# V of the second attention laid out one head over 128 partitions, PV on 128x32 tiles, shared buffer pools, and loads that read 8192 B at once

## The chip, the cores and the metric

The kernel runs on one core of a Trainium2 chip. Its time is the device time of one execution in microseconds (us). A difference is judged on the median of several runs. The profile that is shown is of one execution of the program.

## The reference, cut to what matters

Two attention blocks with cached keys and values are computed on inputs of their own, and their outputs are joined along the last axis. They differ in the number of key heads: the first has 4, each shared by 8 query heads, the second has 32, one for each query head. All inputs are bfloat16.

```python
# first (A): B, Sq, D = 16, 32, 1024; Hq, Hkv, Sk, Dh = 32, 4, 1024, 128
# second (B): the same with H = 32 heads in k_cache and v_cache
q = (x @ wq).reshape(B, Sq, Hq, Dh).transpose(0, 2, 1, 3)
k, v = repeat(k_cache, Hq // Hkv, axis=1), repeat(v_cache, Hq // Hkv, axis=1)
p = softmax(einsum("bhqd,bhkd->bhqk", q, k) * Dh ** -0.5)
o = einsum("bhqk,bhkd->bhqd", p, v)
out = o.transpose(0, 2, 1, 3).reshape(B, Sq, Hq * Dh) @ wo
# result: concatenate([out_A, out_B], axis=-1)
```

K and V of the second attention are 134.2 MB each, those of the first 16.8 MB each. The four weights are 8.4 MB each, x and the result are small. Everything is read once: some 338 MB.

## The kernel before, in words

**Quads.** The work on each attention is cut into 128 quads of 128 score rows: 4 heads or batch entries of 32 queries each, against 1024 keys. A quad of the first attention is 4 query heads that share a key head. A quad of the second takes 2 batch entries and 2 of 4 neighbouring heads (heads e and e + 2 for e = 0, 1), so each of its four groups of 32 rows has keys and values of its own. Two quads of the second attention (e = 0 and 1) make a pair, and `pairB(n)` (line 1209) writes its steps out; `quadA_all` (line 1239) does so for a quad of the first. The main loop (line 1331) goes over 128 steps and puts a quad of each, and parts of the projections, into each step.

**Steps of a quad.** Scores by TensorE into two banks of PSUM (`st_scoresA` line 995, `st_scoresB` line 1027 on 32x32 tiles); row maximum by VectorE (line 1038); exponential with row sum by ScalarE into a buffer P (line 1051); transposes of P by TensorE, two bfloat16 values as one float32 (`st_ptr` line 1063, `st_ptB` line 1097); copy from PSUM into a buffer PT (line 651, on ScalarE or VectorE); PV, the product with the values (`st_pvA` line 1083, `st_pvB` line 1116); scaling by the reciprocal of the row sum into a buffer O (lines 1174 and 1175); a transpose of O (line 1182, line 1190 for the second attention) and a copy into OTA_sb or OTB_sb (line 651); and, once a group of heads is complete, the output projection (line 823) with addition to an accumulator (lines 835 and 844). K of the first attention is transposed by TensorE (line 969), that of the second in place by VectorE (line 976).

**V of the second attention before.** A load (`st_dmaVB`, line 955) brings 512 KB: two neighbouring heads of one batch entry, each over 64 partitions, 16 keys or 4096 B in each partition. Six such tiles lie in VB_sb. PV is done for the pair at once, on four tiles of 64x64: 64 rows of keys, 64 columns of queries (two heads at a time), against 256 columns, the values of both heads. Half of that product belongs to the other head. The unwanted half is left out when O is transposed, by two products with a matrix `rowsel` that holds the identity's rows of one head each:

```python
# line 1116, for c in 16 chunks, t_ in 2 batch entries, q in the pair (e0 = 64 * q.e, n0 = 64 * t_)
last = e.matmul(bank(q.vbo)[n0:n0 + 64, 0:2 * Dh]..., pt2_chunk(vPT, c, e0, n0),
                v2[e0:e0 + 64, :, c, :], start=(c == 0), stop=(c == 15), tile_position=(e0, n0))
# line 1190
for i in range(2):
    last = e.matmul(bank(vb)[:, 256:384], O2_sb[:, vO.idx, i, :], rowsel[:, i, :], start=(i == 0), stop=(i == 1))
```

The last pair has a step of its own (`st_last`, line 1123), which goes over the values in two halves (line 1135); its values lie in tiles of K that are free by then. In the last part of the run V and K also use space of xT_sb, QT_sb and wq_sb that is free by then.

**Buffers.** The quads of the first attention have two P, two PT and two O of their own; a pair of the second has one double P (`P2`), two PT of half the keys for both quads (`PT2`) and three double O (`O2`). PSUM has eight banks that all steps share.

**Loads.** All come from the queue of SP, in order: a load waits at the head of the queue until the last reader of its buffer is done, and what stands behind it waits too. K of the second attention comes in 512 KB tiles of 4096 B rows (line 910, eight tiles in KB_sb), K and V of the first in 256 KB with 2048 B rows (lines 891 and 898, two buffers each), output weights in 256 KB with 2048 B rows (lines 795 and 805), x likewise (line 659), query weights in 512 KB with 2048 B rows (line 714). The outputs go out from GpSimd's queue (line 847) and, the last ones, from SP's (line 841).

**Order.** A planner in the kernel (`list_schedule`, line 249) sets the order of the instructions on each engine when the program is built. It simulates the engines with durations from a table (`DUR`), charges TensorE for going into and out of tiled matmuls (`PE_MODE`, `MODE_IN`, `MODE_OUT`), the loads by their row length (`PACKET`) and their issue (`DMA_ISSUE`), lets SP run at most 5 us ahead of the loads (`SP_AHEAD`), and gives out the buffers of each pool (`SLOTS`) as they come free. Its priorities come from a list of variants (`RANKS`), of which `TUNE` picks one for every 77 operations.

Of the kernel before, what the change touches and what calls it, by code (L numbers as in the profile page):

```python
# [7 lines left out]
ALU = alu_op_type.AluOpType  # L8
# [8 lines left out]
NVB_SLOTS = 6  # L17
XT_FREE = 54
LATE = 51
# [11 lines left out]
PE_MODE = {"scoresB": 2, "Qshuf": 2, "Qshuf2": 2, "PVB": 3, "PVBh": 3}  # L31
MODE_IN = 0.094
MODE_OUT = {0: 0.0, 2: 0.18, 3: 0.1}
PE_INSTR = {"scoresB": 32, "scoresA": 2, "PT_trA": 8, "PT_trB": 8, "PVA": 16, "PVB": 32, "PVBh": 32, "OT_tr": 2, "OT_trB": 4, "KTA_tr": 16, "Qshuf": 16, "Qshuf2": 16,
# [12 lines left out]
TUNE = (6, 7, 1, 5, 6, 8, 8, 8, 8, 8, 8, 11, 5, 15, 1, 9, 0, 1, 5, 1, 7, 14,  # L47
        15, 12, 12, 10, 12, 12, 15, 3, 12, 14, 7, 13, 13, 13, 13, 13, 7, 6, 10, 1, 12, 10,
        3, 12, 0, 11, 9, 12, 7, 13, 12, 11, 12, 3, 4, 10, 14, 9, 9, 10, 4, 0, 0)
# [11 lines left out]
    "scoresB": (0.232, 0.20), "scoresA": (0.216, 0.20), "PT_trA": (0.48, 0.22), "PT_trB": (0.48, 0.22), "PVA": (0.45, 0.22), "PVB": (0.437, 0.22), "PVBh": (0.22, 0.22),  # L61
    "OT_tr": (0.056, 0.22), "OT_trB": (0.112, 0.22), "KTA_tr": (0.45, 0.22), "Qshuf": (0.39, 0.20), "Qshuf2": (0.235, 0.20), "qprojA": (0.432, 0.20), "qprojB": (0.432, 0.20),
    "oprojA": (0.432, 0.20), "oprojB": (0.432, 0.20), "xT_tr": (0.45, 0.22),
    "exp": (1.10, 0.12), "PT_ev@act": (0.466, 0.13), "norm@act": (0.25, 0.13), "normB@act": (0.36, 0.13), "OT_ev@act": (0.11, 0.13), "OTB_ev@act": (0.17, 0.13), "KTA_ev@act": (0.466, 0.13),
    "qA_ev@act": (0.47, 0.13), "qB_ev@act": (0.478, 0.13), "QR_ev@act": (0.478, 0.13), "acc0@act": (0.47, 0.13), "acc0@dve": (0.58, 0.12), "xT_ev@act": (0.90, 0.13),
    "o_fin@act": (0.47, 0.13),
    "KBt_tr": (1.15, 0.11), "max": (1.12, 0.11), "recip": (0.06, 0.11), "norm@dve": (0.265, 0.13), "normB@dve": (0.40, 0.13), "PT_ev@dve": (0.58, 0.12),
    "OT_ev@dve": (0.13, 0.12), "OTB_ev@dve": (0.2, 0.12), "KTA_ev@dve": (0.58, 0.12), "QBt_tr": (0.345, 0.10), "acc+": (0.58, 0.12), "accF": (0.59, 0.12),
# [46 lines left out]
SLOTS = {"bank": 8, "P": 2, "P2": 1, "PT": 2, "PT2": 2, "stat": 8, "O": 2, "O2": 3}  # L115
# [12 lines left out]
class Prog:  # L128
# [120 lines left out]
    def list_schedule(self, lat=0.05, look=LOOK):  # L249
# [170 lines left out]
        while True:  # L420
# [49 lines left out]
            if op.dma_key is not None:  # L470
                free[beng] = st + DMA_ISSUE
# [81 lines left out]
def build(nc, pa, pb, out):  # L553
# [34 lines left out]
    with stack:  # L588
# [21 lines left out]
        VB_sb = sb("VB_sb", [P, NVB, 16 * Dh], BF)  # L610
# [4 lines left out]
        P2_sb = sb("P2_sb", [P, SLOTS["P2"], 2 * Sk], BF)  # L615
        PT2_sb = sb("PT2_sb", [P, SLOTS["PT2"], Sk], BF)
        O2_sb = sb("O2_sb", [P, SLOTS["O2"], 2, Dh], BF)
        rowsel = sb("rowsel", [P, 2, P], BF)
# [19 lines left out]
        pr.add("pool", lambda g: g.memset(rowsel[:], 0.0), writes=["rowsel"], name="c0")  # L638
        for r_ in range(4):
            pr.add("pool", lambda g, r_=r_: g.tensor_copy(rowsel[32 * r_:32 * r_ + 32, r_ % 2, 32 * r_:32 * r_ + 32], ident[32 * r_:32 * r_ + 32, 32 * r_:32 * r_ + 32]),  # L640
                   reads=["ident"], writes=["rowsel"], name="c1")

# [11 lines left out]

        def xT_stage(pi):
            xst = acc[:, pi, :, :].rearrange("p g d -> p (g d)").bitcast(BF)[:, 0:NG * D].rearrange("p (g d) -> p g d", g=NG)
            accres = [("acc", pi, G, oh) for G in range(NG) for oh in range(NOH)]
            for tc in range(NG):
                pr.add("sp", lambda e, tc=tc: e.dma_start(xst[:, tc, :], xfs[pi][tc * P:(tc + 1) * P, :]),
# [743 lines left out]
```

## Time and profile before

| | |
|---|---|
| time, median of 3 runs | 851.15 us (849.29, 851.15, 852.24) |
| profiled execution | span of 849.5 us from its first to its last instruction; no time around the span is listed for it |
| TensorE, weight loads | 783.0 us (92%), 522.6 us (62%) |
| VectorE, ScalarE, GpSimd | 727.0 us (86%), 623.6 us (73%), 6.1 us (1%) |
| moved by the DMA | 341.68 MB, mean 402 GB/s |
| granted TensorE clock | 0.995 |

In rows of groups stand: line, engine, operation, what is written and what is read, shape and count, then busy time in us and mean ns of one instruction, then the engine's idle time just before it and what ended most of it. Busy time counts overlapping instructions once, so tiled matmuls, which overlap, have a busy time far under count times mean. PEld is TensorE's loading of weights, SPq the queue of SP. In rows of stretches each engine's busy time is followed by its number of instructions, and at the end stand granted clock, the share of the 16 DMA engines in use, and GB/s. In rows of waits stand the total in us, the number of waits and the longest.

### The profile page before, as it was taken

To read this page: it belongs to the slowest core of one execution; us is meant where nothing else is said; L and a number is where in the kernel's file an instruction comes from. 1 tells how busy PE (TensorE), PEld (TensorE's weight loads), DVE (VectorE), ACT (ScalarE), POOL (GpSimd) and SP (SyncE) were. 2 spreads that over 40 slices of the span, in tenths; PEclk is the share of its full clock that TensorE was granted. 3 is DMA by queue.
4 is the path that set the end of the run, shared out by engine and by line. 5 is a ranking of instruction groups with operands and counts; after the bars stand their busy time and mean duration, and the time that the engine had idled before them with its cause. 6 is when DMAs were issued, how large, how long until landed. Compare 5 with 4: busy or idle time off the path is not lost.

```text
span 849.5 us, 29749 instructions
## 1 busy us (share of the span) xinstructions
PE 783.0 (92%) x13056; PEld 522.6 (62%) x13056; DVE 727.0 (86%) x1018; ACT 623.6 (73%) x1363; POOL 6.1 (1%) x20
## 2 busy tenths in 40 slices
PE   7989999999898999998999988999899998899878
PEld 4456665666565566665666665666666666666655
DVE  1499987979799898987999898998999978998995
ACT  3497787778677777786788787677877867686874
POOL 1000000000000000000000000000000000000000
PEclk9999999999999999999999999999999999999999
DMA  9999999999999999999999999999999999999995
GB/s 339 415 412 414 411 411 410 405 393 394 416 384 412 409 395 415 416 398 412 414 392 408 411 392 416 415 416 405 410 402 415 412 414 415 415 400 414 416 418 226
DMA packets 112208, 341.68 MB, mean 402 GB/s; under 512 B 12048, under 2 KB 12304, under 8 KB 112080
## 3 DMA queue, kind: packets, MB, share of 16 engines
q1 hardware_dynamic: 111520, 337.95, 100.0%
q8 instruction: 103, 1.69, 0.7%
q0 software_dynamic: 560, 1.84, 0.5%
q14 instruction: 25, 0.20, 0.1%
HBM read 337.64 MB, written 2.10 MB: 400 GB/s over the span
## 4 chain that ended last, share of the span: by engine, by line
PE 55%; DVE 23%; ACT 14%; DMA 5%; issue 2%; SPq 1%; DVEq 0%; ACTq 0%
DVE stat L1038 10%; PE psum L1116 10%; PE psum L823 10%; DVE KB_sb L976 8%; ACT P_sb L1051 8%; PE psum L1027 6%; PE psum L1063 5%; PE psum L754 5%; PE psum L1097 5%; PE psum L1083 4%; DMA KB_sb<-in_B_k_cache_dram 4%; PE psum L995 4%; PE psum L735 4%; ACT PT_sb L651 2%; ACT O_sb L1174 1%
## 5 line engine op out<-in xcount | busy, mean ns | idle before, releaser
L1038 DVE TENSOR_REDUCE stat<-psum 128x1 f32<-128x1024 f32 x256 | 303.6, 1210 | 50.7 <-PE psum L995 31.5
L1051 ACT ACTIVATE P_sb<-psum,stat 128x1024 bf16<-128x1024 f32 x246 | 275.9, 1122 | 63.2 <-DVE stat L1038 59.7
L976 DVE STREAM_TRANSPOSE KB_sb<-KB_sb 128x1024 f32<-128x1024 f32 x240 | 286.6, 1222 | 6.2 <-DMA KB_sb<-in_B_k_cache_dram 6.0
L651 ACT COPY PT_sb<-psum 128x512 f32<-128x512 f32 x226 | 131.4, 604 | 35.2 <-PE psum L1063 22.0
L1116 PE MATMUL psum<-VB_sb,PT_sb 64*64 64x256 bf16 x3584 | 116.2, 271 | 8.6 <-ACT P_sb L1051 5.2
L1116 PEld LDWEIGHTS psum<-VB_sb,PT_sb 64*64 64x64 bf16 x3584 | 97.0, 107 | 27.7 <-issue 25.5
L1174 ACT ACTIVATE O_sb<-psum,stat 128x128 bf16<-128x128 f32 (+1 forms) x205 | 80.8, 417 | 43.2 <-PE psum L1083 23.1
L1063 PE MATMUL psum<-id,P_sb 128*128 128x128 f32 x512 | 88.7, 297 | 6.9 <-ACT P_sb L1051 4.1
L1063 PEld LDWEIGHTS psum<-id,P_sb 128*128 128x128 f32 x512 | 74.0, 208 | 25.2 <-ACT P_sb L1051 13.8
L995 PE MATMUL psum<-KTA_sb,QT_sb 128*128 128x512 bf16 x256 | 84.4, 384 | 3.1 <-ACT P_sb L1051 1.6
L1083 PE MATMUL psum<-VA_sb,PT_sb 128*128 128x128 bf16 x1024 | 78.8, 221 | 7.5 <-ACT P_sb L1051 2.6
L1083 PEld LDWEIGHTS psum<-VA_sb,PT_sb 128*128 128x128 bf16 x1024 | 63.2, 99 | 31.6 <-issue 12.0
L1027 PE MATMUL psum<-KB_sb,QR 32*32 32x512 bf16 x3840 | 73.3, 394 | 8.1 <-ACT P_sb L1051 4.6
L1097 PE MATMUL psum<-id,P_sb 128*128 128x128 f32 x472 | 76.2, 287 | 4.1 <-ACT P_sb L1051 3.5
L754 PE MATMUL psum<-wq_sb,xT_sb 128*128 128x512 bf16 x256 | 72.4, 394 | 3.3 <-DMA wq_sb<-in_B_wq_dram 1.6
L1097 PEld LDWEIGHTS psum<-id,P_sb 128*128 128x128 f32 x472 | 63.8, 193 | 17.3 <-ACT P_sb L1051 7.5
L823 PE MATMUL psum<-woB_sb,OTB_sb 128*128 128x512 bf16 x256 | 66.9, 380 | 2.4 <-ACT P_sb L1051 1.7
L1027 PEld LDWEIGHTS psum<-KB_sb,QR 32*32 32x32 bf16 x3840 | 43.8, 89 | 35.3 <-ACT P_sb L1051 8.3
L823 PE MATMUL psum<-woA_sb,OTA_sb 128*128 128x512 bf16 x256 | 62.8, 380 | 0.4 <-ACT OTA_sb L651 0.3
L735 PE MATMUL psum<-xT_sb,wq_sb 128*128 128x512 bf16 x192 | 54.2, 380 | 1.7 <-issue 1.2
L1051 ACT ACTIVATION_READ_ACCUMULATOR P_sb<-psum,stat 128x1 f32 x246 | 50.3, 205 | 0.0
L835 DVE TENSOR_TENSOR acc<-acc,psum 128x512 f32<-128x512 f32 x64 | 41.3, 675 | 9.6 <-PE psum L823 9.4
(74 smaller groups left out, 720.2 us busy)
## 6 DMA issues: line engine op xcount, KB each, us to landing
KB_sb<-in_B_k_cache_dram SPq DMA_DIRECT2D x240, 512.0 KB, 8.9
VB_sb<-in_B_v_cache_dram SPq DMA_DIRECT2D x234, 512.0 KB, 7.8
KA_sb<-in_A_k_cache_dram SPq DMA_DIRECT2D x64, 256.0 KB, 7.8
VA_sb<-in_A_v_cache_dram SPq DMA_DIRECT2D x64, 256.0 KB, 8.0
wq_sb<-in_B_wq_dram SPq DMA_DIRECT2D x16, 512.0 KB, 8.3
woB_sb<-in_B_wo_dram SPq DMA_DIRECT2D x32, 256.0 KB, 8.5
woA_sb<-in_A_wo_dram SPq DMA_DIRECT2D x32, 256.0 KB, 7.0
wq_sb<-in_B_k_cache_dram SPq DMA_DIRECT2D x16, 512.0 KB, 11.5
```

The costliest lines, as they stand in the source:

```text
L651: return e.copy(dst, src) if hasattr(e, "activation") else e.tensor_copy(dst, src)
L754: last = e.matmul(bank(v)[:, 0:CW], xT_sb[:, 1, j, G * P:(G + 1) * P], wq_sb[:, j, mh * CW:(mh + 1) * CW], start=(j == 0), stop=(j == DJ - 1))
L823: last = e.matmul(bank(v)[:, 0:OUTW], OT[:, gp, hh, :], wo_[:, hh, oh * OUTW:(oh + 1) * OUTW], start=(hh == 0), stop=(hh == nh - 1))
L976: pr.add("dve", lambda e: e.transpose(tile_k(x).bitcast(F32), tile_k(x).bitcast(F32)), writes=[home_k(x)], name="KBt_tr", rtag={home_k(x): ...
L995: pr.add("pe", lambda e, u=u: e.matmul(bank(vS[u]), qt[:, q.b, q.hh0:q.hh0 + 4, :].rearrange("p a q -> p (a q)"), KTA_sb[:, sl, u * 512:(u ...
L1027: last = e.matmul(bank(q.vS[g2])[32 * x:32 * x + 32, :].rearrange("p (s j) -> p s j", s=16), lhsT, rhs, start=(fp == 0), stop=(fp == 3), t ...
L1038: pr.add("dve", lambda e: e.tensor_reduce(stat[:, vst.idx, 0:1], both(vS), AXIS.XY, ALU.max, negate=True), writes=vS + [vst], name="max")
L1051: return e.activation(dst, src, ACTF.Exp, bias=stat[:, vst.idx, 0:1], scale=1.0, accum_out=stat[:, vst.idx, 1:2])
L1063: last = e.transpose(bank(vb)[:, m * P:(m + 1) * P], p32[:, m:Sk // 2:NPK], id32[:])
L1083: last = e.matmul(bank(vb)[:, 0:Dh], ptc_of(vPT, c, 0, P), VA_sb[:, kvs, c, :], start=(c == 0), stop=(c == NCH - 1))
L1097: last = e.transpose(bank(vb)[:, m * P:(m + 1) * P], p32[:, 4 * h + m:Sk:8], id32[:])
L1116: last = e.matmul(bank(q.vbo)[n0:n0 + 64, 0:2 * Dh].rearrange("p (i d) -> p i d", i=2), pt2_chunk(vPT, c, e0, n0), v2[e0:e0 + 64, :, c, :] ...
```

## The change

V of the second attention is loaded a head at a time: 256 KB over 128 partitions, 8 keys or 2048 B in each, four loads for a quad. VB_sb holds three quads of four such tiles, in as many bytes as before. PV is done a quad at a time on four tiles of 128x32: 128 rows of keys, the 32 queries of one head, 128 columns of its values, 8 chunks. Nothing of the product is unwanted, so `rowsel`, the double buffers and the pair's own steps go, and O is transposed as in the first attention. P, PT and O become pools of 4, 4 and 6 for both attentions. `st_last` goes; the last two quads run through the same steps as the others, with their values in halves of free K tiles.

A new helper, `by_four`, writes a load as an instruction whose source is 32 rows of 8192 B and whose destination is 128 rows of 2048 B in 128 partitions. It is used for V of the second attention, K and V of the first, the output weights and x; not for query weights, nor for K of the second attention, which keeps its 4096 B rows. The second attention's output projection takes its heads in the order 0, 2, 1, 3. The planner's tables and its `TUNE` list are replaced, so the order of instructions is another one on every engine.

```diff
-NVB_SLOTS = 6
+NVB_SLOTS = 3
-PACKET = {"kb_dma": (4096, 0.1592), "vb_dma": (4096, 0.1592), "outh_dma": (1024, 0.049), "wqh_dma": (1024, 0.049)}
-PACKET_DEFAULT = (2048, 0.0847)
-DMA_ISSUE = 0.45
+PACKET = {"kb_dma": (4096, 0.1592), "wq_dma": (2048, 0.0847), "out_dma": (2048, 0.0847), "outh_dma": (1024, 0.049)}
+PACKET_DEFAULT = (8192, 0.317)
+ISSUE = {"kb_dma": 0.45, "wq_dma": 0.45, "out_dma": 0.45, "outh_dma": 0.45}
+DMA_ISSUE = 0.62
...
-SLOTS = {"bank": 8, "P": 2, "P2": 1, "PT": 2, "PT2": 2, "stat": 8, "O": 2, "O2": 3}
+SLOTS = {"bank": 8, "P": 4, "PT": 4, "stat": 8, "O": 6}
...
-        VB_sb = sb("VB_sb", [P, NVB, 16 * Dh], BF)
+        VB_sb = sb("VB_sb", [P, NVB, 4, NCH * Dh], BF)
...
+        def wide(e, dst, src):
+            return e.add_instruction(mybir.InstDMACopy(name=nc.get_next_instruction_name(), engine=e.engine, ins=e.lower_ap_dma(src), outs=e.lower_ap_dma(dst),
+                                                       queue="qSPDynamicHW", mode="Copy", cce_op=mybir.AluOpType.bypass, debug=nc.get_debug_info()))
+
+        def by_four(e, dst, rows):
+            return wide(e, dst, rows.rearrange("(c r) d -> c (r d)", c=32))
...
-            pr.add("sp", lambda e: e.dma_start(KA_sb[:, sl, :, :], pa["k"][q.b, q.s].rearrange("(p c) d -> p c d", c=NCH)),
+            pr.add("sp", lambda e: by_four(e, KA_sb[:, sl, :, :].rearrange("p c d -> p (c d)"), pa["k"][q.b, q.s]),
...
-            pr.add("sp", lambda e: e.dma_start(tile_v(x), tile_src("v", x)), writes=[(kind, sl)],
-                   dma_key=f"{kind.lower()}{sl}", name="vb_dma", dur=2 * Sk * Dh * 2, wtag={(kind, sl): ("V", x)})
+            for x in (1, 0, 3, 2):
+                r_ = res_v(t, x)
+                pr.add("sp", lambda e, x=x: by_four(e, tile_v(t, x), pb["v"][q.b0 + x // 2, q.m * MS + 2 * (x % 2) + q.e]), writes=[r_], dma_key=f"{'vl' if kind == 'KB' else kind.lower()}{sl}", name="vb_dma",
+                       dur=Sk * Dh * 2, wtag={r_: ("V", t, x)})
...
+                for c in range(NCH):
+                    for x in range(4):
+                        last = e.matmul(bank(vb)[32 * x:32 * x + 32, 0:Dh], ptc_of(vPT, c, 32 * x, 32 * x + 32), tile_v(q.t, x)[:, c * Dh:(c + 1) * Dh],
+                                        start=(c == 0), stop=(c == NCH - 1), tile_position=(0, 32 * x))
...
+            for q in qs:
+                st_ptr(q)
+                st_pev(q)
             for q in qs:
+                st_pvB(q)
+                while v_next[0] < min(V_LAST, q.t + 1 + NVB + (2 if n >= LATE else 0)):
+                    st_dmaVB(v_next[0])
+                    v_next[0] += 1
                 st_recip(q)
                 st_norm(q)
                 st_otr(q)
```

More of the change, by code (lines that the diff above doesn't have):

```diff
@@ L470, in list_schedule @@
             if op.dma_key is not None:
-                free[beng] = st + DMA_ISSUE
+                free[beng] = st + ISSUE.get(op.name, DMA_ISSUE)
                 xs = max(st + DMA_FIRST, dma_free[0])
@@ L1271, in build @@
         st_dmaVA(quadsA[newA[0]])
-        for x in range(4):
-            st_dmaVB(x)
+        for t in range(2):
+            st_dmaVB(t)
         wo_loadB(0)
@@ L1281, in build @@
             st_dmaKA(quadsA[newA[2]])
-        for x in range(4, NVB):
-            st_dmaVB(x)
+        for t in range(2, NVB):
+            st_dmaVB(t)
         qprojB(0, 0)
```

237 lines of the change are left out of this document (80 added, 157 removed).

## The prediction

> **What bounds the kernel now.** I read the page's busy line and DMA lines first, then stretches of the span one by one, then what the load queue on SP waits for, then the groups of instructions that the change replaces.
>
> ```profile
> span 849.5 us, 29749 instructions
> ...
> PE 783.0 (92%) x13056; PEld 522.6 (62%) x13056; DVE 727.0 (86%) x1018; ACT 623.6 (73%) x1363; POOL 6.1 (1%) x20
> ...
> DMA  9999999999999999999999999999999999999995
> GB/s 339 415 412 414 411 411 410 405 393 394 416 384 412 409 395 415 416 398 412 414 392 408 411 392 416 415 416 405 410 402 415 412 414 415 415 400 414 416 418 226
> DMA packets 112208, 341.68 MB, mean 402 GB/s; under 512 B 12048, under 2 KB 12304, under 8 KB 112080
> ```
>
> The DMA digits are 9 in every slice but the last: the transfers are busy from the first microseconds to about ten before the end. TensorE at 92% and VectorE at 86% are close behind, but each still has time left. The rate moves between 384 and 418 GB/s, and the stretches below say why.
>
> ```profile
> core 0: us, PE busy (x) PEld busy (x) DVE busy (x) ACT busy (x) POOL busy (x), PEclk, DMA share, GB/s
> 10.00:18.00 8.00, 7.30 (x67) 4.86 (x66) 1.83 (x3) 4.28 (x6) 0.00 (x0) 1.00 1.05 407
> 20.00:40.00 20.00, 19.68 (x111) 9.04 (x110) 7.79 (x7) 6.82 (x14) 0.00 (x0) 1.00 1.03 416
> 38.00:46.00 8.00, 6.62 (x114) 3.53 (x114) 7.71 (x8) 6.57 (x13) 0.00 (x0) 1.00 1.05 407
> 40.00:240.00 200.00, 186.09 (x3149) 123.12 (x3159) 176.11 (x248) 155.50 (x338) 0.00 (x0) 0.99 1.03 408
> 240.00:440.00 200.00, 189.10 (x3198) 126.83 (x3167) 178.02 (x249) 149.75 (x327) 0.00 (x0) 1.00 1.02 404
> 440.00:640.00 200.00, 187.67 (x3094) 125.38 (x3092) 178.50 (x253) 149.62 (x331) 0.00 (x0) 1.00 1.03 409
> 640.00:830.00 190.00, 171.14 (x3072) 119.50 (x3070) 174.46 (x241) 145.43 (x327) 2.84 (x5) 0.99 1.03 413
> 840.00:850.00 10.00, 5.95 (x150) 3.30 (x147) 3.63 (x8) 1.42 (x6) 0.54 (x1) 0.93 0.15 56
> ```
>
> The first row is the start, where x and the query weights arrive in rows of 2048 B (the SP rows of that time stand further down): 407 GB/s. The second is mostly K and V of the second attention, rows of 4096 B: 416. The third holds first-attention K and output weights in 256 KB loads, 2048 B rows again: 407. So the row's length sets the rate. From the shapes in the reference 52.4 MB (K and V of the first attention 33.5, output weights 16.8, x 2.1) and 16.8 MB of query weights come in 2048 B rows, and 268.4 MB (K and V of the second attention) in 4096 B rows: 268.4/416 + 69.2/407 = 645.2 + 170.0 = 815 us, a mean of 414 GB/s. The stretch from 40 to 830 us moved (200·408 + 200·404 + 200·409 + 190·413)/790 = 408.4, so 790·(1 − 408.4/414) = 11 us of it are gaps in which the queue ran thin. The last row shows 10 us after the loads in which almost nothing is moved. Hence 849.5 = 815 for the rows, 11 of gaps, 10 of tail, and some 13 for the start, instruction fetches and stores. The times of the runs shown are 849.29 to 852.24 with median 851.15; the profiled span lies 1.65 us under the median, and I carry that difference over unchanged.
>
> **Term 1, the rows.** In time of one of 16 engines, 4096 B at 416/16 = 26.0 GB/s take 157.5 ns, and 2048 B at 407/16 = 25.4 take 80.5. The difference per row is 2·80.5 − 157.5 = 3.5 ns fixed, with 154.0 ns for 4096 B of data. A row of 8192 B would take 2·154.0 + 3.5 = 311.5 ns, 420.8 GB/s. The change reads 8192 B at once for V of the second attention (134.2 MB, 4096 B before) and for the 52.4 MB above, but the row that is *written* into a partition is 2048 B in all of them: for V shorter than now, for the others as now. The trace holds no transfer whose read and written rows differ, so the price has two ends:
> - the read row sets it: V 134.2/416 − 134.2/420.8 = 322.6 − 318.9 = 3.7 us less, the others 52.4/407 − 52.4/420.8 = 128.7 − 124.5 = 4.2 less; together −7.9;
> - the written row sets it: V 134.2/407 − 134.2/416 = +7.1, the others 0; together +7.1.
>
> I take −5: a read row is one fetch from memory, fewer of them are left on every one of these loads, and part of the fixed 3.5 ns will stay with the written row. The nearest row for the others is 407 on both sides, from which they can only rise; V is the one that can fall. The planner in the changed code assumes 0.317 us for 8192 B, against 0.1592 for 4096 and 0.0847 for 2048, which is on the side of a gain; it is an assumption of the code, not a measurement shown here.
>
> **Term 2, more loads on SP.** V comes in 512 loads of 256 KB where it came in 256 of 512 KB; SP gets 1002 loads for 746.
>
> ```profile
> 1.65 1.96 SPq L714 DMA_DIRECT2D wq_sb<-in_B_wq_dram  x4
> 5.69 1.88 SPq L659 DMA_DIRECT2D acc<-in_B_x_dram  x3
> ...
> 404.02 1.75 SPq L955 DMA_DIRECT2D VB_sb<-in_B_v_cache_dram  x4
> 406.73 0.33 SPq L891 DMA_DIRECT2D KA_sb<-in_A_k_cache_dram  x1
> 407.10 0.43 SPq L898 DMA_DIRECT2D VA_sb<-in_A_v_cache_dram  x1
> ```
>
> One issue takes 0.33 to 0.44 us in the middle of the run. 746·0.44 = 328 us of SP now; then 1002·0.44 = 441, or, at the 0.62 that the planner assumes for the new loads (712 of them; 290 as now), 441 + 128 = 569. SP has 849, so this is free as long as it isn't held up. But a 256 KB load lasts 0.63 us at 416 GB/s: while SP issues V at 0.62 it cannot rebuild a lead that it lost; now it gains 1.26 − 0.44 = 0.82 us with each. The rate itself isn't hurt by the smaller load: the third stretch (256 KB loads) runs at the 407 of the first (mostly 512 KB). I put 0 here and the danger into the next term.
>
> The Trainium skill speaks against this edit: in "DMA: Bandwidth & Descriptors", section "Rules for kernel authors", it asks for at least 1 MiB per load and for coalescing. By that rule the 2% between 407 and 416 would belong to the load's size, and V would fall to 407. The equal first and third stretches speak against it here.
>
> **Term 3, the gaps.** What SP waited for:
>
> ```profile
> SPq L955 <- PE psum L1116: 109.9, 36, 6.9
> SPq L910 <- PE psum L1027: 57.0, 24, 5.1
> ```
>
> L955 is the load of V; it waits for the PV matmuls (L1116) to be done with the buffer, up to 6.9 us, and behind it in the queue stand the K loads (L910) and those of the first attention. Now V has six tiles of 512 KB and a pair of heads needs four at once, all released together when its PV ends. Afterwards there are three slots of 1 MB, each released by the PV of one quad, in the same 24 KB per partition: the third slot is always ahead, and a wait covers 1 MB and not 2. PV also ends sooner (term 4). What then ends the wait last is the second quad's PV, or the K tile behind the scores of L1027. Of the 11 us of gaps I take 2.5 back. Ends: all but 3 (−8), and, where SP can't catch up, twice as many gaps (+11); the nearest row, the 109.9 of which many waits lie ahead of need, favours a small gain.
>
> **Term 4, the engines.** These are the groups that are replaced, and those that stand for what comes:
>
> ```profile
> L1116 PE MATMUL psum<-VB_sb,PT_sb 64*64 64x256 bf16 x3584 | 116.2, 271 | 8.6 <-ACT P_sb L1051 5.2 <-issue 2.5 <-ACT KTA_sb L651 0.4
> L1135 PE MATMUL psum<-KB_sb,xT_sb 64*64 64x128 bf16 x128 | 2.0, 217 | 0.0
> L1083 PE MATMUL psum<-VA_sb,PT_sb 128*128 128x128 bf16 x1024 | 78.8, 221 | 7.5 <-ACT P_sb L1051 2.6 <-ACT PT_sb L651 1.8 <-ACT xT_sb L1051 0.9
> L1174 ACT ACTIVATE O_sb<-psum,stat 128x128 bf16<-128x128 f32 x123 | 46.0, 378 | 25.9 <-PE psum L1083 23.1 <-DVE stat L1165 2.2 <-issue 0.2
> L1174 ACT ACTIVATE O_sb<-psum,stat 128x256 bf16<-128x256 f32 x82 | 36.5, 475 | 17.2 <-PE psum L1116 14.3 <-PE psum L995 1.4 <-DVE stat L1165 1.2
> L1190 PE MATMUL psum<-rowsel,O_sb 128*128 128x128 bf16 x252 | 28.3, 222 | 2.9 <-ACT O_sb L1174 2.0
> ```
>
> PV now: 116.2/3584 = 32.4 ns of busy time per matmul of 256 columns, 4032 of them (one pair is done at L1135) = 131 us. Then: 4096 matmuls of 128 columns. L1135 has tiled matmuls of 128 columns at 2.0/128 = 15.6 ns, so 64 us, 67 less, if four 128x32 tiles run side by side as four 64x64 tiles do. If they ran one after another, L1083's 78.8/1024 = 77 ns per matmul would give 315 us. The 64x64 rows are nearer: their column halves overlap already. The product with rowsel (252 matmuls) becomes 128 transposes, some 14 us less. Every pass into and out of tiled matmuls may wait; the order of the changed kernel enters PV 102 times against 78, a few us. TensorE thus falls from 783 to some 705. Scaling the output falls from 475 to 378 ns on 128 quads, 12 us over ACT and DVE. The P and PT buffers of both attentions become pools of four: no new wait in itself, since as many bytes are held.
>
> On the time this is worth nothing directly: the busy DMA hides it all, and its cover is not in doubt, as the work gets less. It is worth something at the end:
>
> ```profile
> L955 SPq DMA_DIRECT2D KB_sb<-in_B_v_cache_dram x4: 431/1004/1060, 822.2 to 824.7; - x4
> DMA to landing us min/median/max: 14.4/15.2/16.1
> 840.43 1.75 PE L1135 MATMUL psum<-KB_sb,xT_sb 64*64 64x128 bf16 x109
> ```
>
> The last V is issued at 824.7 and lands near 839; from there the last PV (2.0 us for the pair), scaling, transpose, output projection and store make the tail. With PV a quad at a time, only 0.5 us of PV and one quad's scaling lie behind the last landing: −1.5, between 0 and −3.
>
> **Sum.** −5 + 0 − 2.5 − 1.5 = −9: a span of 840.5, and a median of 851.15 − 9 = 842.
>
> **Rivals.**
> 1. *Written rows give back what read rows bring* (term 1 near 0, gaps unchanged): only the tail is left, −1.5, 849.6. For it: no row in the trace has unequal sides. Against: the 52.4 MB can't get slower by it. Chance 0.12.
> 2. *The transfer is cut by its shorter side, the 2048 B that a partition receives.* Then nothing is read at 8192 B in effect, V falls from 416 to 407, +7.1, the first attention gains nothing, the tail −1.5: 851.15 + 5.6 = 857. It decides as soon as a written row costs as much as a packet costs now. That is also the case in which the change doesn't do what it says. Chance 0.17. (The Trainium skill's rule above would end at the same time, by another cause.)
> 3. *SP becomes the bound after each wait*: 0.62 us to issue 0.63 us of data, so gaps double, +11, with half of term 1: −2.5 − 1.5 + 11 = +7, 858. For it: waits up to 6.9 us at the head of the queue. Against: 569 of 849 us, and K loads bring 1.26 us of data for 0.44. Chance 0.09.
> 4. *128x32 tiles run one after another*: TensorE 783 − 131 + 315 − 14 = 953 busy, some 960 in all. Against: the overlap of 64x64 tiles. Chance 0.02.
> My forecast keeps 0.60.
>
> **How the numbers follow.** About 0.3%, 2.6 us, is what a measurement of this kernel can tell from no change. Faster by more than that is the forecast, 0.60; rival 1 is the same, 0.12; rivals 2 to 4 are slower, 0.28. The best end is −7.9 − 8 − 3 = −19, 832. The range goes from 832 to 858, which takes in rivals 1 to 3; outside it are rival 4 and mishaps added to rivals 2 and 3. The forecast's own range is 832 to 848.
>
> **What would show it.** In the changed profile: the count of packets (V in 8192 B packets: 16 thousand where there were 33; if cut by the short side, 66); the rate in slices without gaps, 418 or more if I am right, under 412 if rival 2 is; the dips of the GB/s line fewer, or deeper under rival 3, with V issues of 0.62 us back to back in the SP rows; PV near 16 ns per matmul and TensorE near 705 us busy. I am wrong if the steady rate falls, or if it rises and the dips or another engine eat it up.

## The result, and the profile after

The changed kernel takes 846.22 us (median; 843.0 to 848.61) where the kernel before takes 851.15. The ratio is 0.9947 with a 95% interval of 0.9932 to 0.9962: 4.5 us faster, 3.2 to 5.8. One of the eleven runs of the kernel before took 1076.65 us, far from the others, and is left out. The direction was forecast, the size was not: 9 us had been expected. The medians below come from several chips, each with runs of the kernel before beside it, so I compare ratios and give them in us of 851.15.

The page after, with the lines that answer to those shown of before:

```profile
span 844.4 us, 29426 instructions
...
PE 729.9 (86%) x12731; PEld 475.3 (56%) x12864; DVE 721.3 (85%) x1030; ACT 606.0 (72%) x1347; POOL 5.0 (1%) x15
...
DMA  8999999999999999999999999999999999999995
GB/s 334 421 416 410 391 405 417 418 409 391 417 418 403 418 414 419 406 379 414 417 417 401 412 414 417 405 390 414 418 417 416 402 413 416 418 416 417 416 420 229
DMA packets 80720, 341.68 MB, mean 405 GB/s; under 512 B 16144, under 2 KB 16400, under 8 KB 57808
```

Packets fall from 112208 to 80720 although 4096 small ones were added, so V is moved in packets of 8192 B and isn't cut by its shorter side. TensorE is 53 us less busy. The ten best slices ran at 415 to 418 GB/s before and run at 417 to 421 now, but the dips are still there (391, 391, 379, 390). The same stretches as before:

```profile
20.00:40.00 20.00, 19.51 (x109) 8.83 (x109) 7.46 (x7) 6.70 (x14) 0.00 (x0) 1.00 1.03 421
38.00:46.00 8.00, 6.37 (x126) 4.47 (x127) 8.00 (x8) 7.64 (x15) 0.00 (x0) 1.00 1.02 421
40.00:240.00 200.00, 176.90 (x3227) 118.27 (x3260) 175.47 (x254) 154.68 (x347) 0.00 (x0) 0.98 1.02 409
240.00:440.00 200.00, 176.29 (x3033) 114.67 (x3064) 179.09 (x263) 141.57 (x314) 0.00 (x0) 0.98 1.02 410
440.00:640.00 200.00, 180.03 (x3137) 118.48 (x3168) 175.94 (x244) 152.02 (x345) 0.00 (x0) 0.99 1.02 410
640.00:830.00 190.00, 153.95 (x2982) 101.73 (x3006) 174.99 (x251) 136.72 (x310) 2.84 (x5) 0.97 1.02 415
```

The stretch from 20 to 40 us, mostly K and V of the second attention, runs at 421, it was 416. The short stretch with first-attention K and output weights runs at 421, it was 407. From 40 to 830 us the mean is (200·409 + 200·410 + 200·410 + 190·415)/790 = 410.9, it was 408.4. TensorE is busy 8 to 17 us less in each long stretch, and the loads gain little from it.

SP's queue, waits and issues. The first two rows of waits are the kernel before's, for K and V of the first attention. The others are the changed kernel's, where L648 is the helper's line and stands for every wide load (one that reads 8192 B at once):

```profile
SPq L891 <- PE psum L969: 80.9, 34, 6.7
SPq L898 <- PE psum L1083: 54.2, 15, 8.3
...
SPq L648 <- PE psum L1101: 99.2, 38, 6.5
SPq L648 <- PE psum L1124: 28.1, 27, 4.1
SPq L909 <- PE psum L1031: 12.1, 10, 4.6
SPq L648 <- PE psum L976: 10.0, 7, 5.2
SPq L648 <- PE psum L1088: 4.1, 4, 2.1
```
```profile
407.61 4.94 SPq L648 DMA_DIRECT2D VB_sb<-in_B_v_cache_dram  x8
414.24 2.01 SPq L909 DMA_DIRECT2D KB_sb<-in_B_k_cache_dram  x4
418.94 5.18 SPq L648 DMA_DIRECT2D VB_sb<-in_B_v_cache_dram  x8
```

The wait for PV of the second attention (L1101) is nearly as long as before, 99.2 us for 109.9. The other waits have nearly gone: behind the scores of the second attention (L1031) 12.1 us for 57.0, behind the K transposes of the first (L976) 10.0 for 80.9, behind its PV (L1088) 4.1 for 54.2. A V load of 256 KB is issued in 4.94/8 = 0.62 us, where one of 512 KB took 0.44: V of one pair holds SP for 5 us where it held it for 1.75. Added up over the two traces, SP's issues of loads and stores took 383 us and the time between them, mostly waits, 463 us; now it is 637 and 204. It seems that SP waits less because it comes later.

The engines' groups, and the tail:

```profile
L1101 PE MATMUL psum<-VB_sb,PT_sb 128*32 128x128 bf16 x3584 | 67.5, 220 | 4.5 <-ACT P_sb L1056 2.0 <-ACT PT_sb L642 0.6 <-ACT OTA_sb L642 0.4
L1124 PE MATMUL psum<-ident,O_sb 128*128 128x128 bf16 x256 | 51.2, 226 | 15.3 <-ACT O_sb L1117 9.8 <-DVE O_sb L1118 3.9
L1117 ACT ACTIVATE O_sb<-psum,stat 128x128 bf16<-128x128 f32 x221 | 78.3, 371 | 67.4 <-DVE stat L1109 24.0 <-PE psum L1088 21.7 <-PE psum L1101 18.5
```
```profile
838.46 0.63 PE L1101 MATMUL psum<-KB_sb,xT_sb 128*32 128x128 bf16 x32
```

PV takes 67.5/3584 = 18.8 ns of busy time per matmul of 128 columns, so the four 128x32 tiles do run side by side. The last PV starts at 838.46, 5.9 us before the end of the span; before, it started at 840.43, 9.1 us before the end.

### The profile page after: what moved, and what is told of

Read it like the earlier page. It is cut to its first block, busy times and chain, and to the rows that moved or that the text cites. A ratio compares the mean times of both kernels' runs of the same rounds, so it can differ in the third digit from the quotient of the medians.

```text
span 844.4 us, 29426 instructions
## 1 busy us (share of the span) xinstructions
PE 729.9 (86%) x12731; PEld 475.3 (56%) x12864; DVE 721.3 (85%) x1030; ACT 606.0 (72%) x1347; POOL 5.0 (1%) x15
## 2 busy tenths in 40 slices
DMA packets 80720, 341.68 MB, mean 405 GB/s; under 512 B 16144, under 2 KB 16400, under 8 KB 57808
## 4 chain that ended last, share of the span: by engine, by line
PE 43%; DVE 33%; ACT 16%; DMA 4%; issue 3%; SPq 1%; DVEq 0%; ACTq 0%
DVE stat L1043 14%; DVE KB_sb L983 13%; ACT P_sb L1056 10%; PE psum L1068 9%; PE psum L822 8%; PE psum L1031 5%; PE psum L1101 5%; PE psum L733 4%; PE psum L1088 3%; PE psum L1002 3%; PE psum L752 3%; DVE acc L834 2%; ACT PT_sb L642 2%; PE psum L1124 2%; ACT O_sb L1117 2%
## 5 line engine op out<-in xcount | busy, mean ns | idle before, releaser
L1117 ACT ACTIVATE O_sb<-psum,stat 128x128 bf16<-128x128 f32 x221 | 78.3, 371 | 67.4 <-DVE stat L1109 24.0
L1031 PE MATMUL psum<-KB_sb,QR 32*32 32x512 bf16 x3840 | 78.2, 409 | 19.6 <-ACT P_sb L1056 8.8
L1088 PE MATMUL psum<-VA_sb,PT_sb 128*128 128x128 bf16 x1024 | 76.3, 221 | 12.1 <-ACT OTB_sb L642 2.5
L1088 PEld LDWEIGHTS psum<-VA_sb,PT_sb 128*128 128x128 bf16 x1024 | 63.3, 99 | 29.0 <-issue 13.0
L1002 PE MATMUL psum<-KTA_sb,QT_sb 128*128 128x512 bf16 x202 | 67.1, 380 | 10.2 <-issue 2.7
L1101 PE MATMUL psum<-VB_sb,PT_sb 128*32 128x128 bf16 x3584 | 67.5, 220 | 4.5 <-ACT P_sb L1056 2.0
L1031 PEld LDWEIGHTS psum<-KB_sb,QR 32*32 32x32 bf16 x3840 | 44.4, 89 | 44.4 <-ACT P_sb L1056 17.7
L752 PE MATMUL psum<-wq_sb,xT_sb 128*128 128x512 bf16 x230 | 64.4, 390 | 4.9 <-DMA wq_sb<-in_B_wq_dram 1.6
L822 PE MATMUL psum<-woB_sb,OTB_sb 128*128 128x512 bf16 x236 | 62.5, 379 | 6.7 <-ACT P_sb L1056 2.4
L1101 PEld LDWEIGHTS psum<-VB_sb,PT_sb 128*32 128x32 bf16 x3584 | 51.3, 97 | 27.4 <-issue 13.6
L1124 PE MATMUL psum<-ident,O_sb 128*128 128x128 bf16 x256 | 51.2, 226 | 15.3 <-ACT O_sb L1117 9.8
L1124 PEld LDWEIGHTS psum<-ident,O_sb 128*128 128x128 bf16 x256 | 23.7, 99 | 46.6 <-ACT O_sb L1117 27.8
L733 PE MATMUL psum<-xT_sb,wq_sb 128*128 128x512 bf16 x172 | 47.1, 379 | 2.2 <-issue 1.0
```

Of the source, the lines that this page charges most:

```text
L822: last = e.matmul(bank(v)[:, 0:OUTW], OT[:, gp, hh, :], wo_[:, hh, oh * OUTW:(oh + 1) * OUTW], start=(hh == 0), stop=(hh == nh - 1))
L1002: pr.add("pe", lambda e, u=u: e.matmul(bank(vS[u]), qt[:, q.b, q.hh0:q.hh0 + 4, :].rearrange("p a q -> p (a q)"), KTA_sb[:, sl, u * 512:(u ...
L1031: last = e.matmul(bank(q.vS[g2])[32 * x:32 * x + 32, :].rearrange("p (s j) -> p s j", s=16), lhsT, rhs, start=(fp == 0), stop=(fp == 3), t ...
L1088: last = e.matmul(bank(vb)[:, 0:Dh], ptc_of(vPT, c, 0, P), VA_sb[:, kvs, c, :], start=(c == 0), stop=(c == NCH - 1))
L1101: last = e.matmul(bank(vb)[32 * x:32 * x + 32, 0:Dh], ptc_of(vPT, c, 32 * x, 32 * x + 32), tile_v(q.t, x)[:, c * Dh:(c + 1) * Dh], start=( ...
L1117: return e.activation(dst, src, ACTF.Copy, scale=stat[:, vst.idx, 2:3])
```

## The experiments

My theory after the result: the first attention's rows gained, V's did not, and the gaps are made by the engines and by SP, not by the rows. The rivals: the read row pays in full and the gaps have grown; the written row sets the price and the gain is the engines'. (A gap is time in which the queue has too few loads in flight, and a dip is a slice of the GB/s line in which that shows.)

### What a row costs

The kernel before, with the wide read for K and V of the first attention, output weights and x alone:

```diff
-e.dma_start(KA_sb[:, sl, :, :], pa["k"][q.b, q.s].rearrange("(p c) d -> p c d", c=NCH))
+by_four(e, KA_sb[:, sl, :, :].rearrange("p c d -> p (c d)"), pa["k"][q.b, q.s])   # likewise VA, woA, woB, x
```

> The kernel before, its order of instructions unchanged, with K and V of the first attention, output weights and x read at 8192 B; V of the second attention as before. If reads set the price: 52.4 MB from 407 to 421, 4.2 us less, 847. If both sides cost: 407 to 416, 3 us less, 848. If writes set it, or the transfer is cut by its shorter side: 851.

Measured: 848.75, ratio 0.9978 (0.9959 to 0.9996), 1.9 us less. Its stretch from 38 to 46 us:

```profile
38.00:46.00 8.00, 7.02 (x114) 3.54 (x114) 7.57 (x7) 6.62 (x12) 0.00 (x0) 1.00 1.03 422
```

The rate there rises to 422 with the written row still at 2048 B. The changed kernel has 421 there, and 406 with all its rows plain (the second of the next two runs). So in this kernel the written row does not set the price, and rival 2 of the prediction is out.

The changed kernel with V in plain rows, and with all wide reads in plain rows:

```diff
-by_four(e, tile_v(t, x), pb["v"][...])
+e.dma_start(tile_v(t, x), pb["v"][...].rearrange("(p c) d -> p (c d)", c=NCH))
```
```diff
-return wide(e, dst, rows.rearrange("(c r) d -> c (r d)", c=32))
+return e.dma_start(dst, rows.rearrange("(c r) d -> c (r d)", c=P))
```

> The changed kernel, its order unchanged, with V of the second attention read in plain 2048 B rows; the others at 8192 B. If the wide read is what keeps V at 416: 134.2 MB at 407, 7 us more than the changed kernel, 853. If reads alone set the price: 10 us more, 857. If writes set it: no difference, 846.

> The changed kernel, its order unchanged, with every wide read turned into plain 2048 B rows; what is left of the change is the layout of V, PV on 128x32 tiles, the pools and the order. If both sides cost: 7 + 3 = 10 us more than the changed kernel, 856. If reads alone: 14 more, 860. If writes: 846. Should it come out under 851, the layout and the pools gain more than the rows.

Measured: 851.82, ratio 1.0015 (1.0001 to 1.0030); and 856.3, ratio 1.0072 (1.0056 to 1.0089). In the changed order the wide read is thus worth 0.57%, 4.8 us, on the first attention's loads (with output weights and x), and 0.68%, 5.8 us, on V, each against 2048 B. A wide load also takes SP longer: V loads start 0.64 us apart, plain ones 0.48 (medians of the traces), so the rows by themselves may be worth more. With plain rows throughout, what is left of the change is 6.1 us slower than the kernel before. For V the plain row is not the comparison with before, where it came in 4096 B rows. The next run makes that one:

```diff
-rows.rearrange("(c r) d -> c (r d)", c=32)   # V only
+rows.rearrange("(c r) d -> c (r d)", c=64)
```

> The changed kernel, its order unchanged, with V of the second attention read in rows of 4096 B, written in 2048 as in the changed kernel: the read row of before with the written row of after. If the price is the read row's: between the changed kernel and the one with plain rows, two thirds of the way down from 851.8, so 848. If V neither gained nor lost because the written row took what the read row brought: 849 to 850. If the length of the read row plays no part in itself: 851 to 852, or 846.

Measured: 845.69, ratio 0.9948 (0.9929 to 0.9966), the changed kernel's own 0.9947. My 848 was wrong: in time, V gains from 2048 to 4096 B and, within some 2 us, nothing from there to 8192, with loads 0.64 us apart in both. V had 4096 already. The kernel before with K and V of the second attention at 8192:

```diff
-e.dma_start(tile_k(x), tile_src("k", x))
+wide(e, tile_k(x), tile_src("k", x).rearrange("(c r) x -> c (r x)", r=2))   # V likewise
```

> The kernel before, its order unchanged, with K and V of the second attention (268 MB) read in rows of 8192 B and written in rows of 4096 as now; the first attention as before. If the read row sets the price: 268.4/416 - 268.4/421 = 7.6 us less, 843.5. If the written row does: 851. If both cost as in my theory: 2 to 4 less, 848.

Measured: 849.11, ratio 0.9979 (0.9958 to 1.0001): most likely 1.8 us less, no difference within the interval, and not the 7.6 of the full read-row price. The rate is another matter:

```profile
GB/s 343 418 403 420 408 405 383 416 394 395 420 373 408 412 399 417 421 409 415 407 396 414 414 382 421 420 409 403 412 407 409 415 420 417 419 418 412 420 422 216
...
20.00:40.00 20.00, 19.66 (x110) 8.80 (x108) 7.57 (x7) 6.33 (x13) 0.00 (x0) 1.00 1.02 422
40.00:240.00 200.00, 181.09 (x3095) 122.94 (x3127) 174.28 (x247) 154.42 (x337) 0.00 (x0) 0.99 1.01 404
240.00:440.00 200.00, 186.66 (x3171) 127.04 (x3203) 179.15 (x250) 150.85 (x329) 0.00 (x0) 1.00 1.01 406
440.00:640.00 200.00, 183.67 (x3060) 125.31 (x3092) 178.38 (x252) 149.53 (x331) 0.00 (x0) 1.00 1.01 409
640.00:830.00 190.00, 168.19 (x3108) 119.18 (x3130) 175.62 (x243) 145.48 (x328) 2.84 (x5) 1.00 1.02 417
```

From 20 to 40 us, mostly K and V of the second attention, it ran at 422 GB/s where the kernel before had 416, and the best slices reach 420 to 422: the read row pays from 4096 to 8192 B too, about as the prediction worked out (420.8). But the dips are deeper, down to 373, 382 and 383 where the kernel before had 384, 392 and 392, and the mean from 40 to 830 us is 408.9 for 408.4. So the gaps took back what the rows gained, and my theory that V's rows gained nothing holds for the time and not for the rate. These wide loads also took SP longer, 0.64 us from one V load to the next for 0.48.

### Loads by themselves

> A kernel of loads alone: it leaves out the whole computation and stores zeros. Seven stretches of 37.7 MB each, one after another, with all buffers free: a) 512 KB, read and written in 4096 B rows, b) 256 KB, 2048 B both, c) 256 KB, read 8192, written 2048, d) 512 KB, read 8192, written 4096, e) 256 KB, read 4096, written 2048, f) 512 KB, read 16384, written 4096, g) 256 KB, read 16384, written 2048. If the read row alone sets the price: a 416 GB/s, b 407, c 421, d 421, e 416, f and g 423. If the written row alone: c, e and g 407, d and f 416. If both cost (my theory now: the first attention's loads gained, V neither gained nor lost): c 415 to 417, d 418 to 420, e 410 to 413.

> Loads alone once more (the whole computation is left out, zeros are stored), now with 4 MB issued ahead, as much as in the two kernels, and with their mixes. Ten stretches: 1) 512 KB, 4096 B read and written; 2) 512 KB, 2048 both; 3) 256 KB, 8192 read, 2048 written; 4) 256 KB, 2048 both; 5) 512 KB, 8192 read, 4096 written; 6) the mix before: 8 of the first kind to 2 of the fourth; 7) the same with the two of the third kind; 8) the mix after: 4 of the first, 10 of the third; 9) 4 of the first, 10 of the fourth; 10) 4 of the fifth, 10 of the third. If the load's size sets the price: 2 equals 1, and 8 equals 9, both under 6. If the written row does: 2, 3 and 4 equal, 8 equals 9. If both rows cost, as the timed runs say: 8 within 1 of 6, 9 some 8 GB/s lower, 7 some 2 higher than 6.

The kernel of loads with 4 MB ahead (so much is issued before the oldest has landed), its first four stretches in order, then the mix after and the mix after with plain rows:

```profile
20.00:68.00 48.00, 0.00 (x0) 0.00 (x0) 1.00 1.03 410
90.00:148.00 58.00, 0.00 (x0) 0.00 (x0) 1.00 1.05 387
170.00:228.00 58.00, 0.00 (x0) 0.00 (x0) 1.00 1.02 388
250.00:305.00 55.00, 0.00 (x0) 0.00 (x0) 1.00 1.05 387
...
545.00:600.00 55.00, 0.00 (x0) 0.00 (x0) 1.00 1.02 396
620.00:675.00 55.00, 0.00 (x0) 0.00 (x0) 1.00 1.04 398
```

By itself the price is the written row's: 410 GB/s for 4096 B, 387 for 2048, in loads of 512 KB and 256 KB alike, and whether 2048 or 8192 are read. The first load-only kernel, with all buffers free, showed the same 410 and 387 (and some 254 for read rows of 16384 B that leave 16 rows to a load). That contradicts the full kernel, where the wide read reaches 421 and plain rows 407 in the same stretch. Two runs looked for what differs.

> Loads alone (the whole computation is left out, zeros are stored), now from the addresses and in the order of the two kernels, since loads of neighbouring addresses gave 410 and 387 whatever the read row. Eleven stretches: 1) K in 512 KB, 4096 B both; 2) V in 256 KB, 8192 read, 2048 written; 3) V in 256 KB, 2048 both; 4) the mix before (4 K, 4 V of 512 KB, 2 of the first attention); 5) the mix after; 6) the mix after with plain 2048 B rows; 4 MB ahead in all of these; 7) to 9) as 4) to 6) with 2.25 MB ahead; 10) and 11) neighbouring addresses, kinds 1 and 2, 2.25 MB ahead. If the addresses matter: 1 at 415 or more, 5 at 414 to 420 and 6 some 8 below it. If the written row alone sets the price whatever the order: 1 at 410, 2 and 3 at 387, 5 equals 6 at 396; then the gain of the wide reads in the full kernel comes from something that only the full kernel has. If it is the lead: 7 to 9 differ from 4 to 6.

> Loads alone, five stretches twice: 512 KB with 4096 B rows; 256 KB read 8192, written 2048; 256 KB of 2048 both; the mix after; the mix after with plain rows. The first five run beside plain work of TensorE, VectorE and ScalarE that has nothing to do with the loads, the second five without (the computation is left out in both). If the load-only kernels lacked the wide read's gain because the other engines stood still: beside the work 414 to 417 for the first, the mix after some 8 GB/s over the plain one, and 410, 387, 387, 396, 396 without it. If the work plays no part: the same in both halves.

Read inside the stretches, without the first and last microseconds of each: with the kernels' addresses and order 410, 387 and 387 for the first three kinds, 398 for the mix after, 397 with plain rows; with 2.25 MB ahead 395 and 394. Beside the work of three engines the first four stretches ran at 410, 387, 387 and 396, without it at 409, 387, 388 and 398. In the fifth, 397 with and without, TensorE's work had nearly ended. As they were tried here, neither the addresses, nor the lead, nor work beside the loads is it. What lets the wide read gain in the full kernel stays open.

### What the engines' time is worth

The changed kernel with an eighth of PV, and with the maximum over half of the keys:

```diff
-for c in range(NCH):
+for c in range(1):
```
```diff
-both(vS)
+both(vS)[:, :, 0:256]
```

> The changed kernel, its order unchanged, with PV of the second attention for one of the 8 chunks of keys alone (the others are left out): 3584 matmuls less, some 50 us of TensorE's busy time. If TensorE still makes the gaps in the loads: 4 to 8 us less than the changed kernel, 839 to 842. If it doesn't: 845 to 847.

> The changed kernel, its order unchanged, with the row maximum taken over half of the keys (the other half is left out of the maximum alone): some 130 us of VectorE's busy time less. If VectorE's chain of maximum and K transposes now makes the gaps: 5 to 9 us less, 837 to 841. If not: 845 to 847.

Measured: 840.07, ratio 0.9875 (0.9847 to 0.9904), 6.1 us under the changed kernel; and 841.93, ratio 0.9892 (0.9861 to 0.9922), 4.7 under it. In the first of them the loads themselves run faster in the first 400 us:

```profile
40.00:240.00 200.00, 173.41 (x2374) 109.13 (x2397) 181.38 (x260) 158.46 (x357) 0.00 (x0) 0.99 1.02 417
240.00:440.00 200.00, 167.41 (x2210) 103.10 (x2236) 180.70 (x266) 142.09 (x319) 0.00 (x0) 0.99 1.02 415
```

417 and 415 where the changed kernel has 409 and 410, with the same loads in the same order; later it has 409 and 407 for 410 and 415. The DMA shows 9 tenths in all slices of the page but the first and the last, and yet shorter engine work moves the loads: buffers come free earlier, and the queue doesn't run thin. And what is TensorE's lighter work worth in the order before?

```diff
-for c in range(c0, c0 + 4):
+for c in range(c0, c0 + (3 if c0 < 8 else 2)):
```

> The kernel before, its order unchanged, with 10 of the 16 chunks of PV of the second attention (the other 6 are left out, save in the last pair): some 49 us of TensorE's busy time less, about what the change took off TensorE. If TensorE's time makes the gaps before as it does after: 5 to 7 us less, 845; then the change got its few us from the engines and the rows gave little. If the order before hides TensorE's time behind the loads: 850 to 852.

Measured: 845.51, ratio 0.9940 (0.9921 to 0.9959), 5.1 us less. That alone is as much as the whole change brought. Its stretches:

```profile
40.00:240.00 200.00, 180.25 (x2871) 115.01 (x2847) 179.32 (x254) 158.20 (x344) 0.00 (x0) 1.00 1.03 411
240.00:440.00 200.00, 182.29 (x2752) 116.51 (x2750) 179.16 (x253) 150.05 (x331) 0.00 (x0) 1.00 1.03 412
440.00:640.00 200.00, 180.25 (x2823) 116.95 (x2824) 181.62 (x254) 151.00 (x335) 0.00 (x0) 1.00 1.03 412
```

411, 412 and 412 GB/s with all rows as before, where the kernel before had 408, 404 and 409 (and 411 for 413 from 640 to 830 us).

### What SP's time costs

With the engines at 5.1 and the first attention's rows at 1.9, the change should have brought 7. The changed kernel with more time of SP for each V load:

```diff
+if op.name == "vb_dma":
+    for _ in range(10):                    # 42 in the kernel before, below
+        eng.wait_ge(sems["pool"], 1)       # fulfilled long ago
 last = op.emit(eng)
```

> The changed kernel, its order unchanged, with ten waits that are already fulfilled ahead of each V load on SP, some 0.4 to 0.5 us of SP's time for each of the 512. If SP's 0.6 us per V load leaves so little lead that it makes the gaps: 10 us more or far above, 856 and up. If SP has time to spare: 846 to 849.

```profile
408.70 6.51 SPq L651 DMA_DIRECT2D VB_sb<-in_B_v_cache_dram  x8
```

Measured: 850.67, ratio 1.0000 (0.9983 to 1.0018), 4.5 us more than the changed kernel, for 6.51/8 − 0.62 = 0.19 us of each load. The ten waits took less than the expectation said, and they cost less than half of its least, for 512·0.19 = 97 us of SP. So SP's time is not free, though SP still stands waiting for part of the run. Put into the kernel before, where SP's time for V was to become that of the changed kernel:

> The kernel before, its order unchanged, with 42 waits that are already fulfilled ahead of each V load on SP, some 0.8 us for each 512 KB. With its own 0.43 that is the 1.24 us that SP needs for 512 KB of V in the changed kernel, with everything else as before. If SP's issue time took part of the gain: 2 to 5 us more, 853 to 856. If SP has time to spare: 850 to 852.

```profile
409.85 5.24 SPq L958 DMA_DIRECT2D VB_sb<-in_B_v_cache_dram  x4
```

Measured: 862.77, ratio 1.0133 (1.0116 to 1.0150), 11.3 us more, far over my 2 to 5. Part of that is my edit, which slowed SP more than I meant: the row has three sets of waits between four loads, and one issue takes 0.33 us, so from one V load to the next it is (5.24 − 0.33)/3 = 1.64 us, where 1.24 was the aim and 0.48 stood before. For 256·1.16 = 297 us of SP, 11.3 us are 0.04 for each us; the 4.5 for 97 of the run above are 0.05. The two orders thus pay about the same. Half the number of V loads tests it from the other side, in the changed order with plain rows (each load here brings two heads, 512 KB):

```diff
-by_four(e, tile_v(t, x), pb["v"][b, h])                                          # x = 0 and 1, 2 and 3
+e.dma_start(VB_sb[:, sl, x:x + 2, :], pb["v"][b, h:h + 3:2].rearrange("i (p c) d -> p i (c d)", c=NCH))   # x = 0, 2
```

> The changed kernel, its order unchanged, with V in plain 2048 B rows as in the run above with 851.8, but two heads in one load of 512 KB: half as many V loads. If the number of loads and SP's time for them cost: 847 to 850. If only the row length counts: 851 to 852.

```profile
408.15 2.50 SPq L973 DMA_DIRECT2D VB_sb<-in_B_v_cache_dram  x4
```

Measured: 850.57, ratio 0.9981 (0.9969 to 0.9993), against 1.0015 with the same plain rows in 256 KB loads: 2.9 us less. V of a pair takes SP 2.5 us here, and 3.7 with plain loads of 256 KB, so the number of V loads is worth about 3 us with plain rows. With the wide reads of the changed kernel it is 4.9 us, and no run halves that.

### How much the picked order carries

```diff
-TUNE = (7, 15, 14, ...)
+TUNE = (0,) * 65
```

> The changed kernel with the planner's list of variants set to the first one throughout, which gives another order of instructions. If the order found by the list is worth as much as the change: 850 to 860. If the loads set the time whatever the order: 846 to 849.

> The kernel before with the list of variants set to the first one throughout. With an order that was not picked the two kernels compare layout and rows alone: if those are worth the 5 us that were measured, this one is 5 us over the changed kernel with the first variant; if engine time is worth more where the order is worse, 8 to 12 over it; if the picked order made the difference, the same.

Measured: 853.82, ratio 1.0047 (1.0028 to 1.0066), and 884.9, ratio 1.0412 (1.0387 to 1.0437). Without picked variants the two are 31 us apart, not 5. The picked order takes 35 us off the kernel before and 8.5 off the changed one: it seems that most of what the lighter layout is worth had been got already, by an order in which the heavier one fits. That is a reading: the two kernels differ in rows and pools as well.

### A version that might beat both

> A version that might beat both: the changed kernel, its order unchanged, with K of the second attention read at 8192 B too and written in rows of 4096. If the read row still pays beyond 4096: 844 to 845. If it pays only from 2048 to 4096: 846.

Measured: 844.68, ratio 0.9937 (0.9917 to 0.9958), for 0.9947 of the changed kernel: 0.9 us better, within the intervals. It is the fastest complete version here, and not shown to be faster than the changed kernel.

## Why the prediction was right in direction and wrong in size

**What bounds it.** Only in part as read. The loads run all the time, but 11 us of gaps were named and then taken as small change. The runs with less PV (in both orders) and with half the maximum show that engine time moves the time by 5 to 6 us. The page's row of nines hid that: a share of 1.02 to 1.03 stands beside 404 and beside 417 GB/s.

**Where the 5 us of the span came from.** The prediction's own working can be redone for the changed kernel: 186.6/421 + 134.2/416 + 16.8/407 = 807 us for the rows, a mean of 418.3 GB/s, for 815 and 414. The stretches' 410.9 then leaves 790·(1 − 410.9/418.3) = 14 us of gaps, for 11. What is left of the span is 23.4 us in both. So the span is shorter by 8 for the rows and longer by 3 for the gaps: 5.1 together. This is an estimate from one profiled execution of each, and a rate that is off by 0.5 GB/s is 1 us of gaps.

**Term 1, rows, −5.** The read end, −7.9, was the right one for the rate: loads of 8192 B ran at 421 and 422, and V, written in rows of 2048 B, did not slow the stretch from 20 to 40 us (421 for 416). The −5 leaves part of the price with the written row, and the full kernels don't show that part. The time shows less than the rate: the first attention's loads gave 1.9 us in the order before and 4.8 in the one after, for 4.2 worked out, and V from 4096 to 8192 B nothing.

**Term 2, more loads on SP, 0.** This is a step that failed. SP's time was added up (569 of 849 us, free as long as it isn't held up), and V at 0.62 us was seen not to rebuild a lead, yet the price was put at nothing but a chance in a rival. SP was held up already: its issues took 383 us of the run and the time between them 463, and two of its largest sums of waits, 80.9 and 54.2 us, do not appear in the prediction. Half the V loads give 2.9 us back with plain rows, 0.19 us on each costs 4.5, and 1.16 on each in the order before 11.3. Some 3 us of the gain went there by the first of these; how much it is with the wide reads, which take SP longer, stays open. Rival 3 named the mechanism; what it had wrong is that it would turn the sum around.

**Term 3, gaps, −2.5.** This is the other step that failed: by the working above the gaps grew by 3. They were taken as a term of their own, which shrinks whatever the rows do. The runs show that they go together. V read at 4096 B in the changed order (its stretches run at 414, 410, 409 and 414) has 811 us of rows and 9 of gaps, and takes as long as the changed kernel with its 807 and 14. K and V at 8192 B in the order before have 808 and 17, for 815 and 11. When the loads run faster and the engines free the buffers no sooner, the queue runs thin more often. How much of the 3 comes from the faster rows and how much from SP's longer issues is not separated. The reason given for −2.5 was wrong too: the wait for PV hardly shrank (99.2 us for 109.9).

**Term 4 and the tail, −1.5.** The lighter TensorE alone is worth 5.1 us (the kernel before with less PV), more than the 4 of terms 3 and 4 together; "on the time this is worth nothing directly" was wrong. The last PV starts 5.9 us before the end of the span for 9.1, but the 23.4 us outside rows and gaps are the same in both, so that no gain of the tail is shown. TensorE's busy time was put at 705 and is 730: PV at 18.8 ns for 15.6 makes 13 us of that. Another 9 are the transposes of O: 51.2 us (L1124), where the kernel before had 28.1 for those of the first attention and 28.3 for the product with `rowsel`, so 5 less and not 14.

**Sum.** The forecast was −9 and −4.5 was measured. The rows were taken 3 too small, the gaps 5.5 and the tail 1.5 too well. The errors partly cancel, so that the sum is nearer than its terms, and that is luck. The timed runs can be added up too: −1.9 for rows, −5.1 for TensorE and +2.9 for SP make −4.1. But each was measured with an order of its own left as it was, with the rows at 4.8, as in the changed order, they make −7, and that such terms simply add is not shown.

**Rivals.** The tiles run side by side, as said. Rival 1 falls with the rates of 421, and rival 2 with the 422 GB/s of the kernel before with wide rows, and with the packet count. Of the Trainium skill's rule in "DMA: Bandwidth & Descriptors", section "Rules for kernel authors" (large loads, coalesced), I had said that the two stretches at 407 speak against it. For the rate they do: in the load-only kernel 512 KB and 256 KB loads of 2048 B rows both run at 387. For the time the rule's direction was right here, since plain V in 512 KB loads is 2.9 us faster than in 256 KB ones, with 1.2 us less of SP for each pair.

## What to carry to other kernels

A DMA share near 100% does not mean that only bytes count: look at the rate in stretches, and ask for each dip which buffer came free late. A higher rate of the loads and the gaps between them are not separate terms: faster loads can run dry more often, and then the time shows little of the rate. Before splitting loads, multiply their number by the issue time of one, and compare one issue with the time its bytes take; where the two are equal, the queue can never catch up after a wait, and an in-order queue waits often: this one stood waiting for about half of the run before. A kernel whose order was searched for may hide the cost of its layout, so that a better layout shows little of its worth at first.

## What the runs showed of the hardware that I had not expected

In kernels of loads alone the rate follows the row that is written, 410 GB/s for 4096 B and 387 for 2048, whatever row is read up to 8192 B. In the full kernel the same wide loads ran at 421 to 422 and plain ones at 406 to 407, with the same written row of 2048 B, and loads written in rows of 4096 B ran at 422 when read at 8192 and at 416 when read at 4096. Addresses, lead and work beside them did not explain it.

A load whose source rows are longer than its destination's takes SP longer to issue: V loads of 256 KB start 0.64 us apart with 32 source rows of 8192 B and also with 64 of 4096, and 0.48 us apart with 128 plain rows of 2048.
